# An attention and MLP block on one core: the next q asked for in step 2 of a unit, two maxima at the first score tile of every projection step, six pairs held back in one query block

## Chip, core and metric

One core of a Trainium2 chip runs the whole kernel. The metric is the device time of one execution in microseconds (us); the time of a kernel is the median of several executions.

## The reference, cut to what matters

An adaLN block: attention with 16 heads of 28 columns on 2048 tokens of 448 columns, then a channel MLP. Everything is float32.

```python
sa, ca, ga, sb, cb, gb = (mod[:, i] for i in range(6))      # mod = silu(c) @ w_mod
h = _layernorm(x) * (1 + ca) + sa
q, k, v = split(h @ wqkv)                                    # 16 heads of 28
p = softmax(q @ k.T * 28 ** -0.5)
x = x + ga * ((p @ v) @ wo)
h = _layernorm(x) * (1 + cb) + sb
x = x + gb * (gelu(_layernorm(h) @ w1 + b1) @ w2 + b2)
```

## The kernel before

**Phase 1** (to about 168 us) makes q, k and v. Each q and k is kept as two parts, a rounded one (hi) and the rest (lo), and stored in DRAM by group of 4 heads.

**Phase 2** is the attention and the subject here. It has 16 units (NU), unit u = 4 g + qt for head group g and query block qt of 512 queries, and each unit has 16 steps kt, one for each 128 keys; step s = 16 u + kt counts them through. A step makes two score tiles, each of two heads, by 12 matmuls (L1297: hi·hi, hi·lo, lo·hi), ScalarE takes the exponential of each tile (L1310), and the matmuls of the step before's probabilities with v follow (`av`, L1255). A head has 28 rows, so it sits in one of four groups of 32 rows of the TensorE array: the heads j = 0 and 1 of a group are the score tile of half 0, the heads 2 and 3 that of half 1.

The exponential needs each query's maximum before its unit begins. These **maxima** are the filler work of phase 2: a matmul of q and k by the hi parts (L476, row group j) and a VectorE reduction over its 512 keys (L481). 64 of them belong to a query block (4 sub-blocks i of queries, 4 heads j, 4 key chunks cch). The list `mxq` holds those that are left, and `emit_single(half, ...)` takes the next whose operands are there, by preference one of the asked half; a matmul in row groups that the score matmuls beside it don't use can run with them. What is taken, and so the row group, follows from the whole history of the list.

- Up to step 119 (RING) an even step takes two maxima at the first score tile (half 0, so heads 2 and 3 are asked for) and two at the second; an odd step one and two. `n0` (L1285) is the number at the first tile.
- **Pairs** save a reduction: `open_pair` makes the maximum of a difference of two key chunks (ScalarE, L641) in a buffer, `close_pair` (L648, VectorE) turns it into two maxima at once. Only heads 2 and 3 are paired; `PAIR_ROWS` says of how many of the 4 sub-blocks of a query block (the default is all 4, 8 pairs). `kept_back` holds the maxima of coming pairs away from `emit_single`.
- From step 119 on ("ring") a step takes one maximum at the first tile and two in one tile at the second: `emit_pair` looks for two heads of the asked half with the same i and cch, and reduces both at once (L684). If it finds none it makes two single ones in the same tile (L687, reduced at L481).
- The steps kt = 8 to 11 of units 12 to 15 are the **projection steps** (`is_wo`): each carries the output projection of 128 tokens (L396), and three maxima.

When the last maximum of a query block is done, `max_fin` folds them; **`put`** (L523) transposes them on VectorE (L525) and writes them by four small DMAs (L528) into the row of the unit's q tile that the scores read. It runs only when that q tile has been asked for: **`load_q`** (L777, two DMAs of 256 KB, hi and lo, recorded at L770). The hi parts for the maxima of the next head group (`kh`, `qh`) are loaded by `load_hi` (L508) when the last maximum that needs the old ones has been taken; the planner may use a loaded tile 3 steps later (L504).

All these DMAs stand in the one queue of **SyncE (SP)**, in program order, and SP waits at each until what it needs is there. In the same queue stand the DMAs of a unit's end: `den` (L998) in step 1 of the next unit, then `drec` (L1006) and its broadcast `osb` (L1008) in step 4 (step 2 in units 12 to 15), for which GpSimd (POOL) waits at L1013 to normalise; in units 12 to 15 the result goes by L1023 and L1024 into the projection steps.

Of the kernel before, what the change touches and what calls it, by code (L numbers as in the profile page):

```python
# [33 lines left out]
LAST_MAX = NKT - 4  # L34
RING = 119
PAIR_AT = (2, 2, 0, 2)
PAIR_ROWS = {(0, 2): 2, (0, 3): 3, (1, 0): 2, (1, 1): 2}
WO_MAX = 3
YTAGS = [f"{a}{i}" for a in ("kh", "qh") for i in range(4)]
EPS = 1e-5  # L40
# [4 lines left out]
def tile_adaln_block(ctx: ExitStack, tc: tile.TileContext, x, wqkv, wo, w1, b1, w2, b2, c, w_mod, out):  # L45
# [36 lines left out]
    def slot(tag, shape, dt=F32R):  # L82
        return sb.tile(shape, dt, tag="slot_" + tag, name=nm("slot_" + tag), bufs=1)
# [14 lines left out]
    def ps_two(key):  # L98
        return ps_pools[key][1].tile([128, 2, 512], F32, tag=key, name=nm(key), bufs=1)

    def ps_s2():
        s_ring.append(s_ring.pop(0))
        return ps_two(s_ring[-1])
# [4 lines left out]
    def ps_mx():  # L108
        mx_ring.append(mx_ring.pop(0))
        return ps_tile(mx_ring[-1], 1 if mx_ring[-1] == "m1" else 2)  # L110

    def ps_o():
        return ps_tile("o")
# [418 lines left out]
    def tick_late(force=False):  # L532
        for e in late:
            e[0] -= 1
        while late and late[0][2] in qst and (force or late[0][0] <= 0):
            late.pop(0)[1]()
# [74 lines left out]
    def other(m):  # L611
        return m[:2] + (m[2] + 1,) + m[3:]

    def pairable():
        return [
            m for m in mxq
            if m[2] == PAIR_AT[m[0]] and m[4] > 1 and other(m) in mxq and m[3] < PAIR_ROWS.get(m[:2], 4)
        ]
# [26 lines left out]
    def close_pair():  # L645
        (g, qt, cch, i, j), r = px_open.pop()
        p = max_mm(g, qt, i, j, kh_sb[(g, cch)])
        dve.tensor_tensor_reduce(  # L648
            out=r, in0=p, in1=r, scale=1.0, scalar=-3.0e38, op0=ALU.add, op1=ALU.max,
            accum_out=mxp[(g, qt)][:, i, j, cch + 1 : cch + 2],  # L650
        )
        count(g, qt, [cch, cch + 1])

    def emit_single(half, ps):
        near = ready_max()
        if not near:
            return
        whole = {}
        for m in near:
            whole[by_set(m)] = whole.get(by_set(m), 0) + 1  # L660
        fits = [m for m in near if m[4] // 2 == half]
        alone = [m for m in fits if whole[by_set(m)] == 1]
        same = [m for m in fits if m[:2] == near[0][:2]]
        m = (alone or same[-2:] or fits or near)[0]
        if clock[0] < RING:
            kept = kept_back()
            js = [e[0][4] for e in px_open]
            m = min(near, key=lambda x: (x in kept, x[4] // 2 != half, x[4] in js))
        mxq.remove(m)
        g, qt, cch, i, j = m  # L670
        max_one(g, qt, cch, i, j, ps)
        count(g, qt, [cch])

    def emit_pair(half, t):
        near = ready_max()
        for a, m in enumerate(near):
            n = m[:4] + (m[4] + 1,)
            if m[4] == 2 * half and n in near:
                mxq.remove(m)
                mxq.remove(n)  # L680
                g, qt, cch, i, j = m
                for jj in range(2):
                    max_mm(g, qt, i, j + jj, kh_sb[(g, cch)], lambda: t[:, jj])
                dve.tensor_reduce(out=mxp[(g, qt)][:, i, j : j + 2, cch], in_=t, op=ALU.max, axis=AX.X)  # L684
                count(g, qt, [cch, cch])
                return
        for jj in range(2):  # L687
            emit_single(half, lambda: t[:, jj])
# [36 lines left out]
    def finish_max(g, qt):  # L725
        if px_open and px_open[0][0][:2] == (g, qt):
            close_pair()
        while left[(g, qt)] > 0:
            emit_max(1)
# [35 lines left out]
    qst = {}  # L765
# [11 lines left out]
    def load_q(u):  # L777
        g, qt = divmod(u, NB)
        qst[u] = load_parts(f"b{u % 2}", 0, g, slice(qt * 512, (qt + 1) * 512))
# [136 lines left out]
    def third_tile(on):  # L916
        ps_close("m2" if on else "s2")
        ps_open("s2" if on else "m2", "right")
        mx_ring[:] = ["m1"] if on else ["m1", "m2", "m2"]
# [249 lines left out]
    NU = NG * NB  # L1169
# [61 lines left out]
    def is_wo(s_):  # L1231
        return s_ // NKT >= NU - NB and 8 <= s_ % NKT < 12

    def extra(s_):
        if is_wo(s_):
            return False
        most = 0
        need = 0
        for v in range(s_ // NKT + 1, NU):
            need += left.get(divmod(v, NB), 64)  # L1240
            rest = range(s_, NKT * (v - 1) + LAST_MAX)
            n_wo = sum(is_wo(x) for x in rest)
            n_plain = len(rest) - n_wo
            if n_plain > 0:
                most = max(most, (need - 3 * n_plain - WO_MAX * n_wo) / n_plain)
        due[0] += min(most, 1)
        if due[0] < 1:
            return False
        due[0] -= 1
        return True  # L1250
# [12 lines left out]
    for u in range(NU):  # L1263
        g, qt = divmod(u, NB)
        for kt in range(NKT):
            step = u * NKT + kt
            if kt == 6 and u + 1 < NU and u + 1 not in qst:
                load_q(u + 1)
            clock[0] = step
            if kt == LAST_MAX and u + 1 < NU:  # L1270
                finish_max(*divmod(u + 1, NB))
            tick_late()
            if not (three or mxq or late):
                three = True
                s_ring[:] = ["s0", turns[step % 2], turns[1 - step % 2]]
            now[0] = turns[step % 2]
            was, ring = ring, step >= RING and (three or not is_wo(step))
            first = step % 2 if ring else 0
            pt = {hf: slot(tags[step % len(tags)], [128, 2, 512], F32) for hf, tags in zip((first, 1 - first), ptags)}
            if ring != was:  # L1280
                third_tile(ring)
            more = ring and not three and extra(step)
            late_one, after = after, more
            n_max = 0 if ring else WO_MAX if is_wo(step) else 4 - step % 2
            n0 = 1 if step % 4 == 3 else 2  # L1285
            closing = bool(px_open) and step % 2 == 1

            ks, qs = kst[(g, kt // 4)], qst[u]
            kc = slice((kt % 4) * 128, (kt % 4 + 1) * 128)
            for n, hf in enumerate((first, 1 - first)):  # L1290
                s2 = ps_s2() if three else ps_two((now[0] if n else "s0") if ring else ("s1", "s0")[n if step < RING else 1 - n])
                for term, (kp, qp) in enumerate(((0, 0), (1, 0), (0, 1))):
                    if ring and n == 1 and term == 2 and mxq:
                        emit_pair(first, ps_two(turns[1 - step % 2]))
                    for jj in range(2):
                        rows_ = slice(64 * hf + 32 * jj, 64 * hf + 32 * jj + DH + (term == 0))
                        pe.matmul(s2[:, jj, :], ks[rows_, kp, kc], qs[rows_, qp, :], start=(term == 0), stop=(term == 2))  # L1297
                    if closing:
                        if (n, term) == (0, 0):
                            close_pair()  # L1300
                    elif n == 0 and term < n0 <= n_max:
                        emit_single(1, ps_mx)
                    if n == 1 and term == 2:
                        for _ in range(2 if closing else n_max - n0):
                            emit_single(0, ps_mx)
                    if ring and (n, term) == ((1, 0) if late_one else (0, 0)) and not three:
                        emit_single(1 - first, ps_mx)
                    if n == 1 and term == 2 and more:
                        emit_single(first, ps_mx)
                act.activation(pt[hf], s2, AF.Exp, scale=SCALE)  # L1310
            if step == 0:
                v_task(NB - 1, 3, ps_mx())
            if pend is not None:
                pu, pkt, pp, po = pend
                av(pu, pkt, pp, po)
                if pkt == NKT - 1:
                    end_unit(pu, po)
            if step % 2 and step + 2 < RING:
                open_pair()
            if kt == 0:  # L1320
                o = ps_o()
            pend = (u, kt, pt, o)
            if qt == NB - 1 and kt % 4 == 3 and g + 1 < NG:
                load_k(g + 1, kt // 4 if g else kt // 4 ^ 2)
            for fn in sched.pop(step, ()):
                fn()
# [115 lines left out]
```

## Time and profile before

| | us |
|---|---|
| median of 3 runs | 1121.79 |
| lowest and highest | 1120.84, 1122.47 |
| the profiled execution | 1122.83 |
| its span on the core | 1120.9 |
| phase 2, first score matmul to the start of the last step | 168.2 to 822.9 |

The profiled execution's own time is 1.93 us longer than its span, and 1.04 us above the median of the runs. In the rows that the prediction quotes a time is in us from the start of the span. A row of a timeline has start, duration, engine, line, operation, tile and source, the number of instructions merged into the row, and in brackets the idle time before it with what ended it. "SPq" rows are the issue of a DMA on SP. A row of a table of stretches has the stretch, its length, then for PE (matmuls), PEld (weight loads), DVE (VectorE), ACT (ScalarE) and POOL the busy time and the number of instructions, and then the clock that TensorE was granted, as a share of full speed, and the DMA load.

### The profile page before, as it was taken

The page shows a single profiled execution, that of the slowest core. Times are in us where ns is not written, and L with a number is a line of the kernel's source. Part 1 is how long each engine was busy: PE and PEld are TensorE (multiplying, and loading weights), DVE is VectorE, ACT ScalarE, POOL GpSimd, SP SyncE. Part 2 cuts the span into 40 slices and gives each one's busy share as a digit, 9 for nine tenths or more (in the row PEclk, how much of TensorE's full clock was granted, in tenths as well). Part 3 has the DMA queues.
Part 4 walks back from the last instruction along what each step waited for, and adds up shares of the span by engine and source line. Part 5 has one row for each costly group of instructions (what it writes and reads, how often), then busy time and mean ns, then how long its engine had stood idle before and what let it go on. Part 6 is the DMA issues. An engine that isn't in the chain of part 4 may idle for free.

```text
span 1120.9 us, 20683 instructions
## 1 busy us (share of the span) xinstructions
PE 1105.9 (99%) x8319; PEld 669.6 (60%) x8319; DVE 807.3 (72%) x1393; ACT 693.9 (62%) x878; POOL 214.9 (19%) x215
## 2 busy tenths in 40 slices
PE   9999999999999999999899999999999999999998
PEld 6756675444444444444344454545568888888887
DVE  6968788999989989988788867573648853444322
ACT  4555657888888888888788878576752311111210
POOL 2533333010000000000100020206214504023000
PEclk9999999999999999999999999999999999999999
DMA  8563263121132101231211412111322100000000
GB/s 309 200 200 93 88 201 112 31 86 33 56 114 59 57 30 58 58 87 58 76 40 39 143 30 87 57 30 58 91 69 78 31 33 1 1 33 1 33 1 33
DMA packets 49341, 81.19 MB, mean 72 GB/s; under 512 B 12311, under 2 KB 18702, under 8 KB 49234
## 3 DMA queue, kind: packets, MB, share of 16 engines
q1 hardware_dynamic: 48762, 79.14, 22.7%
q8 instruction: 65, 1.06, 0.4%
q10 hardware_dynamic: 148, 0.46, 0.1%
q0 software_dynamic: 336, 0.28, 0.1%
q14 instruction: 30, 0.25, 0.1%
HBM read 55.04 MB, written 26.48 MB: 73 GB/s over the span
## 4 chain that ended last, share of the span: by engine, by line
PE 92%; DVE 3%; DMA 2%; ACT 1%; issue 1%; SPq 0%; POOL 0%; DVEq 0%; ACTq 0%; POOLq 0%
PE s L1297 22%; PE o L1255 22%; PE m L396 16%; PE pa L396 8%; PE m L476 8%; PE s L1377 3%; PE s L1378 3%; PE s L1376 3%; DVE mxp L481 2%; PE s L476 2%; PE t L1377 1%; PE t L1378 1%; PE t L1376 1%; PE ma L476 1%; DMA slot_c<-in_w_mod_dram 1%
## 5 line engine op out<-in xcount | busy, mean ns | idle before, releaser
L481 DVE TENSOR_REDUCE mxp<-m 128x1 f32<-128x512 f32 x564 | 365.8, 686 | 87.4 <-PE m L476 68.6
L1297 PE MATMUL s<-slot_b,slot_a 28*128 28x512 f32 (+1 forms) x3072 | 360.0, 425 | 0.5 <-ACT slot_c0h L1310 0.5
L1297 PEld LDWEIGHTS s<-slot_b,slot_a 28*128 28x128 f32 (+1 forms) x3072 | 212.6, 184 | 172.5 <-ACT slot_c L1310 91.4
L476 PE MATMUL m<-kh,qh 28*128 28x512 f32 x598 | 222.0, 469 | 4.2 <-DMA kh<-d 3.3
L1310 ACT ACTIVATE slot_c<-s 128x1024 f32<-128x1024 f32 x170 | 174.8, 1028 | 57.8 <-PE s L1297 56.2
L1255 PE MATMUL o<-slot_c,v 128*32 128x512 f32 x680 | 179.6, 607 | 0.0
L1353 ACT ACTIVATE full<-m,b_col 128x512 f32<-128x512 f32 x56 | 38.6, 689 | 191.9 <-PE m L396 179.7
L1255 PE MATMUL o<-slot_c1h,v 128*32 128x512 f32 x512 | 136.3, 611 | 0.9 <-ACT slot_c1h L1310 0.9
L1255 PE MATMUL o<-slot_c0h,v 128*32 128x512 f32 x512 | 134.7, 605 | 0.0
L1310 ACT ACTIVATE slot_c0h<-s 128x1024 f32<-128x1024 f32 x128 | 131.4, 1026 | 3.4 <-PE m L396 2.4
L684 DVE TENSOR_REDUCE mxp<-s 128x2 f32<-128x1024 f32 x104 | 127.5, 1226 | 5.1 <-PE s L476 0.6
L1310 ACT ACTIVATE slot_c1h<-s 128x1024 f32<-128x1024 f32 x128 | 130.7, 1021 | 0.0
L1356 DVE CAST hi<-full 128x512 fp32r<-128x512 f32 x56 | 25.2, 450 | 135.1 <-ACT full L1353 135.1
L1310 ACT ACTIVATE slot_d<-s 128x1024 f32<-128x1024 f32 x86 | 88.3, 1027 | 29.1 <-PE s L1297 26.3
L476 PEld LDWEIGHTS m<-kh,qh 28*128 28x128 f32 x598 | 89.8, 182 | 20.6 <-DVE mxp L481 12.3
L1255 PE MATMUL o<-slot_d,v 128*32 128x512 f32 x344 | 91.4, 610 | 0.4 <-ACT osb L1219 0.4
L1013 POOL TENSOR_TENSOR osb<-osb,osb 128x512 f32<-128x512 f32 x16 | 20.9, 1306 | 365.7 <-DMA osb<-drec 306.0
L396 PE MATMUL m<-y,slot_a 128*128 128x512 f32 x160 | 60.7, 395 | 0.0
L648 DVE CUSTOM_DVE_ANT_0 slot_d0i<-m,slot_d0i 128x512 f32<-128x512 f32 x55 | 38.0, 691 | 15.2 <-PE m L476 12.8
L476 PE MATMUL s<-kh,qh 28*128 28x512 f32 x210 | 47.7, 441 | 0.8 <-DVE mxp L481 0.8
L1357 DVE TENSOR_TENSOR lo<-full,hi 128x512 fp32r<-128x512 f32 x56 | 44.1, 788 | 5.2
L1255 PEld LDWEIGHTS o<-slot_c,v 128*32 128x32 f32 x680 | 24.5, 108 | 39.0 <-issue 36.5
(342 smaller groups left out, 1845.6 us busy)
## 6 DMA issues: line engine op xcount, KB each, us to landing
slot_b<-d SPq DMA_DIRECT2D x32, 256.0 KB
slot_a<-d SPq DMA_DIRECT2D x32, 256.0 KB
d<-lo SPq DMA_DIRECT2D x28, 256.0 KB
d<-hi SPq DMA_DIRECT2D x16, 256.0 KB
osb<-drec SPq DMA_DIRECT2D x15, 256.0 KB
out_dram<-xn SPq DMA_DIRECT2D x16, 224.0 KB
raw<-in_B_w_dram SPq DMA_DIRECT2D x14, 224.0 KB
qh<-d SPq DMA_DIRECT2D x12, 256.0 KB
```

Source lines behind the costliest of these rows:

```text
L396: pe.matmul(p, a, b, start=(i == 0), stop=(i == len(terms) - 1))
L476: pe.matmul(m, qh_sb[(g, qt)][js, i * 128 : (i + 1) * 128], k[js, :], start=True, stop=True)
L481: dve.tensor_reduce(out=mxp[(g, qt)][:, i, j, cch : cch + 1], in_=m, op=ALU.max, axis=AX.X)
L684: dve.tensor_reduce(out=mxp[(g, qt)][:, i, j : j + 2, cch], in_=t, op=ALU.max, axis=AX.X)
L1255: pe.matmul(o[32 * j : 32 * j + 32, :], v_sb[kt // 4][:, kt % 4, 4 * g + j, :], p[j // 2][:, j % 2, :], start=(kt == 0), stop=(kt == NKT - 1),
L1297: pe.matmul(s2[:, jj, :], ks[rows_, kp, kc], qs[rows_, qp, :], start=(term == 0), stop=(term == 2))
L1310: act.activation(pt[hf], s2, AF.Exp, scale=SCALE)
L1353: act.activation(gf, p, AF.Gelu_apprx_tanh, bias=b1_col[:, i : i + 1])
L1357: dve.tensor_tensor(out=glo, in0=gf, in1=f(ghi), op=ALU.subtract)
L1376: pe.matmul(pp, ghi[:, ts], w_hi, start=(m == 0), stop=False)
L1377: pe.matmul(pp, ghi[:, ts], w_lo, start=False, stop=False)
L1378: pe.matmul(pp, glo[:, ts], w_hi, start=False, stop=(m == NFT - 1))
```

## The change

Three places are edited; no instruction of a new kind comes in.

```diff
-PAIR_ROWS = {(0, 2): 2, (0, 3): 3, (1, 0): 2, (1, 1): 2}
+PAIR_ROWS = {(0, 2): 2, (0, 3): 3, (1, 0): 2, (1, 1): 2, (1, 2): 3}
...
-            if kt == 6 and u + 1 < NU and u + 1 not in qst:
+            if kt == 2 and u + 1 < NU and u + 1 not in qst:
                 load_q(u + 1)
...
-            n0 = 1 if step % 4 == 3 else 2
+            n0 = 1 if step % 4 == 3 and not is_wo(step) else 2
```

The first holds back the pairs of 3 sub-blocks of the query block (1, 2), 6 pairs, where it were 8. The number of pairs in the program stays 55: block (1, 2) has two fewer, block (2, 2) three where it had one. But it changes what `emit_single` takes from step 54 on, and so the row groups, the steps in which query blocks are finished and those in which `load_hi` runs. Two maxima of heads 0 and 1 stand at the first tile (half 0, the same row groups) of steps 72, 74, 76 and 78 in the kernel before, and of steps 76 and 78 in the changed one; late in unit 14, maxima in the row groups of their tile stand in steps 229 to 232 before, and once, in step 233, after. The second edit moves `load_q`, and with it `put`, ahead of the unit's `drec`. The third changes steps 203 and 219 (kt = 11 of units 12 and 13) alone, since units 14 and 15 have no maxima left by then.

**SP's queue in unit 9** (steps 144 to 159). In the kernel before, from the unit's `den` on; `kh` and `qh` are hi parts of head group 3, `slot_b` with source `d` the q of unit 10 and with source `full` its `put`:

```order
L998 DMA den_7319<-osb_7287 128x1x16
L508 DMA kh_1804_7372<-d_244 128x512
L1006 DMA drec_7413<-den_7319 128x16
L1008 DMA osb_7415<-drec_7413 128x1x512
L770 DMA slot_b_1820_7446<-d_235 128x512
L770 DMA slot_b_1820_7446<-d_239 128x512
L528 DMA slot_b_1820_7446<-full_7449 4x4x32 x4
L508 DMA kh_1826_7463<-d_244 128x512
L508 DMA kh_1847_7566<-d_244 128x512
L508 DMA qh_1849_7571<-d_236 128x512
```

In the changed kernel the same place reads:

```order
L508 DMA kh_1776_7249<-d_244 128x512
L998 DMA den_7321<-osb_7287 128x1x16
L770 DMA slot_b_1793_7323<-d_235 128x512
L770 DMA slot_b_1793_7323<-d_239 128x512
L528 DMA slot_b_1793_7323<-full_7326 4x4x32 x4
L1006 DMA drec_7420<-den_7321 128x16
L1008 DMA osb_7422<-drec_7420 128x1x512
L508 DMA kh_1821_7446<-d_244 128x512
L508 DMA kh_1826_7463<-d_244 128x512
L508 DMA qh_1828_7468<-d_236 128x512
```

The q and its `put` now stand ahead of `drec` and `osb`, and the loads of `kh` directly behind `osb`. In the kernel before the first of the two late `kh` (kh_1826, chunk 3) is asked for in step 150 and first used in step 154; in the changed kernel chunk 2 (kh_1821) is asked for in step 149 and first used in step 152, chunk 3 in steps 150 and 157.

**PE in step 152** of the changed kernel, the first matmuls of the step:

```order
L1255 MATMUL o_7289<-slot_c0h_7456,v_230 32x512 x2
L1297 MATMUL s_1839_7522<-slot_b_1683_6822,slot_a_1639_6629 128x512 x2
L476 MATMUL m_1840_7525<-kh_1821_7446,qh_1400_5645 128x512
L1297 MATMUL s_1839_7522<-slot_b_1683_6822,slot_a_1639_6629 128x512 x4
L1297 MATMUL s_1841_7533<-slot_b_1683_6822,slot_a_1639_6629 128x512 x4
```

and in the kernel before, where the `kh` of that place is one of chunk 0 that was loaded long ago:

```order
L1255 MATMUL o_7289<-slot_c0h_7456,v_230 32x512 x2
L1297 MATMUL s_1837_7517<-slot_b_1711_6948,slot_a_1640_6631 128x512 x2
L476 MATMUL m_1838_7520<-kh_1749_7125,qh_1585_6374 128x512
L1297 MATMUL s_1837_7517<-slot_b_1711_6948,slot_a_1640_6631 128x512 x4
L1297 MATMUL s_1839_7528<-slot_b_1711_6948,slot_a_1640_6631 128x512 x4
```

The third row is the one that moved: the new `kh` is read by the third matmul of the step.

**DVE in unit 14**, steps 229 to 231 (kt = 5 to 7), in the kernel before, where the two single reductions (x2) of one score-sized tile are step 230's:

```order
L481 TENSOR_REDUCE mxp_9310<-m_2388_10076 128x1
L684 TENSOR_REDUCE mxp_9310<-s_2390_10089 128x2
L481 TENSOR_REDUCE mxp_9310<-m_2395_10108 128x1
L481 TENSOR_REDUCE mxp_9310<-s_2397_10121 128x1 x2
L481 TENSOR_REDUCE mxp_9310<-m_2401_10139 128x1
L684 TENSOR_REDUCE mxp_9310<-s_2403_10152 128x2
```

and in the changed kernel:

```order
L481 TENSOR_REDUCE mxp_9419<-m_2389_10079 128x1
L684 TENSOR_REDUCE mxp_9419<-s_2391_10092 128x2
L481 TENSOR_REDUCE mxp_9419<-m_2395_10108 128x1
L684 TENSOR_REDUCE mxp_9419<-s_2397_10121 128x2
L481 TENSOR_REDUCE mxp_9419<-m_2401_10138 128x1
L684 TENSOR_REDUCE mxp_9419<-s_2403_10151 128x2
```

The two single reductions became one over both banks. It is the only such place in either kernel.

## The prediction

> **What bounds the kernel.** I read the page's busy times first, then a table of stretches by unit, then TensorE's waits.
>
> ```profile
> span 1120.9 us, 20683 instructions
> PE 1105.9 (99%) x8319; PEld 669.6 (60%) x8319; DVE 807.3 (72%) x1393; ACT 693.9 (62%) x878; POOL 214.9 (19%) x215
> ...
> 490.00:525.90 35.90, 35.90 (x372) 15.46 (x368) 31.47 (x38) 31.43 (x34) 2.61 (x3) 1.00 0.23 68
> 525.90:567.00 41.10, 37.84 (x375) 16.12 (x371) 31.07 (x38) 31.41 (x34) 3.81 (x3) 0.96 0.20 59
> 567.00:602.80 35.80, 35.80 (x372) 15.40 (x368) 31.21 (x36) 31.37 (x34) 2.61 (x3) 1.00 0.13 39
> ...
> 683.70:701.60 17.90, 17.90 (x191) 7.65 (x187) 15.35 (x18) 15.76 (x18) 1.28 (x1) 1.00 0.18 47
> 731.10:752.40 21.30, 20.52 (x191) 8.80 (x187) 15.52 (x19) 15.86 (x18) 1.26 (x1) 0.92 0.15 40
> ```
>
> TensorE is busy almost throughout, so a change without less matmul work gains only where TensorE stands still or runs slower than it could. The stretches show two such places. Units 8, 9 and 10 do the same work, but unit 9 (the second row) takes 41.1 us where its neighbours take 35.9 and 35.8: **5.2 us** too many. The first 8 steps of unit 14 (last row) take 21.3 us where those of unit 13 take 17.9: **3.4 us** too many. Both have a clock below 1.00. TensorE's waits name the causes:
>
> ```profile
> PE m L476 <- DMA kh<-d: 3.3, 1, 3.3
> ...
> PE s L476 <- DVE mxp L481: 0.8, 1, 0.8
> ```
>
> One wait of 3.3 us for a `kh`, one of 0.8 for a reduction. The rest of the two excesses is the clock. In stretches of 3.41 us around the two waits:
>
> ```profile
> 546.25:549.66 3.41, 2.69 (x29) 1.07 (x25) 2.35 (x4) 2.65 (x3) 0.37 (x1) 1.00 0.09 28
> 549.66:553.08 3.42, 0.88 (x13) 0.76 (x13) 0.38 (x1) 0.11 (x1) 0.00 (x0) 1.00 0.69 207
> 553.08:556.49 3.41, 3.41 (x25) 1.25 (x23) 1.76 (x3) 1.83 (x2) 0.00 (x0) 0.50 0.00 0
> 556.49:559.90 3.41, 3.41 (x42) 1.26 (x34) 3.06 (x5) 2.88 (x4) 1.19 (x1) 1.00 0.13 46
> 744.22:747.64 3.42, 2.64 (x27) 1.28 (x23) 2.46 (x4) 2.29 (x4) 1.26 (x1) 1.00 0.22 65
> 747.64:751.05 3.41, 3.41 (x22) 1.54 (x15) 0.97 (x2) 1.01 (x1) 0.00 (x0) 0.50 0.00 0
> ```
>
> Half clock is granted for exactly one stretch, directly after one with 13 or 27 matmuls; 42 are usual (fourth row), and 29 (first row) had no penalty. A half-clock stretch does 25 matmuls for 42, a loss of 3.41 x (1 - 25/42) = 1.4 us at least; half of it, 1.7 us, is my value; the unit's excess less the wait, 5.2 - 3.3 = 1.9, is the upper end.
>
> **Part 1: the loads of unit 9 (first and second edit).** SP's queue there:
>
> ```profile
> 529.39 0.59 SPq L998 DMA_DIRECT2D den<-osb  x1
> ...
> 537.82 0.32 SPq L1006 DMA_DIRECT2D drec<-den  x1
> 539.23 0.55 SPq L1008 DMA_DIRECT2D osb<-drec  x1
> 539.83 0.95 SPq L770 DMA_DIRECT2D slot_b<-d  x2
> 545.74 2.28 SPq L528 DMA_DIRECT2D slot_b<-full  x4
> 548.07 0.91 SPq L508 DMA_DIRECT2D kh<-d  x2
> ...
> 552.20 0.46 PE L476 MATMUL m<-kh,qh 28*128 28x512 f32 x1 [3.26 <-DMA kh<-d]
> ```
>
> The `put` (L528) cannot issue until the q that it writes into has landed, 545.74 - 539.83 = 5.9 us; then its four issues take 2.3 us, and the `kh` behind them, asked for in step 150, issues at 548.07 and is used at 552.20. In the changed kernel `put` has been served by then: its q issues right behind `den`, at 529.39 + 0.59 = 529.98, and even at 5.9 + 2.3 us SP is free at 538.2, when `drec` is due anyway (537.82). So this wait goes. What is late next is the `kh` of chunk 2. It stands directly behind `osb`, in the place that the q's first DMA has above, so it issues at 539.83; a DMA in that place landed 5.9 us later, and 5.8 us later a unit earlier:
>
> ```profile
> 503.72 0.94 SPq L770 DMA_DIRECT2D slot_b<-d  x2
> 509.53 2.28 SPq L528 DMA_DIRECT2D slot_b<-full  x4
> ...
> 544.01 0.50 PE L1297 MATMUL s<-slot_b,slot_a 29*128 29x512 f32 x2
> ```
>
> That gives 545.7, and step 152, whose third matmul needs it, starts at 544.01: a **new wait of 1.7 us**. Its bounds: 0 if it lands in the 4.1 us that `kh` took without an `osb` ahead (548.07 to 552.20, with 539.83 giving 544.0), and 3.3, the old wait. I take 1.7, since the row that has `osb` ahead is the nearest. Behind the waiting matmul stand the rest of the step's scores, then ScalarE's exponentials: everything waits. In one stretch of 3.41 us this leaves TensorE 1.7 us, about 21 matmuls, fewer than the 27 that were followed by half clock; so I add 1.7 us of clock (0 to 1.9). Unit 9 then costs 3.4 where it cost 5.2: **-1.8 us**. Bounds: -5.2 (no wait, no clock) and 0.
>
> The Trainium skill ("TensorE: Matmul & The Clock Gate", Part 1: The HAM clock gate) speaks against the added clock: its array falls to half rate after at least one idle window of about 3.4 us. The rows agree with the 3.41 us window, but not with the idle time: 0.78 us of idling was enough in unit 14, so here the measurement decides. By that rule of the Trainium skill the sum below would be 1.7 us lower.
>
> **Part 2: unit 14.** In step 230 no two maxima fit one reduction, so two single ones share a tile:
>
> ```profile
> 746.06 0.69 DVE L481 TENSOR_REDUCE mxp<-s 128x1 f32<-128x512 f32 x1
> ...
> 746.80 0.49 PE L476 MATMUL s<-kh,qh 28*128 28x512 f32 x1 [0.78 <-DVE mxp L481]
> ```
>
> The second matmul waits for the reduction of the first (746.06 + 0.69 = 746.75), and the half-clock stretch follows. The changed kernel has the double reduction there, and the steps keep their usual row groups. The excess of 3.4 goes; in exchange step 233 has one maximum in its score tile's rows, 0.1 by part 3. **-3.3 us.** Bounds: -3.4, and -1.7 if half clock comes for another reason.
>
> **Part 3: row groups in unit 4.** A step with free row groups and two of the four with taken ones, from first score matmul to first score matmul:
>
> ```profile
> 340.84:343.62 2.78, 2.78 (x29) 1.36 (x25) 2.75 (x5) 2.75 (x4) 0.00 (x0) 1.00 0.18 49
> 350.97:353.90 2.93, 2.93 (x29) 1.70 (x26) 2.61 (x5) 2.93 (x4) 1.29 (x1) 1.00 0.15 48
> 356.13:359.07 2.94, 2.94 (x29) 1.68 (x25) 2.50 (x6) 2.87 (x4) 0.00 (x0) 1.00 0.02 6
> ```
>
> In the first VectorE is busy 2.75 of 2.78 us: it sets the pace. In the others it has slack, and TensorE makes the same 29 matmuls in 0.15 us more. Steps 72 and 74 lose the conflict, 76 and 78 keep it: 2 x 0.155 = **-0.3 us** (0 to -0.3).
>
> **Part 4: what costs nothing.** Pairs remain 55, so the work of VectorE and ScalarE is the same:
>
> ```profile
> L648 DVE CUSTOM_DVE_ANT_0 slot_d0i<-m,slot_d0i 128x512 f32<-128x512 f32 x55 | 38.0, 691 | 15.2 <-PE m L476 12.8
> ```
>
> The `put` transposes and folds keep their number and move within a unit; VectorE has slack in the ring (31.5 of 35.9 us), and before it they move from one even step to another. The third edit, by the steps kt = 10, 11 and 12 of unit 12:
>
> ```profile
> 665.76:669.93 4.17, 4.17 (x34) 2.58 (x34) 1.89 (x3) 2.47 (x3) 1.15 (x1) 1.00 0.00 0
> 669.93:674.07 4.14, 4.14 (x33) 2.60 (x32) 1.98 (x3) 2.48 (x3) 1.14 (x1) 1.00 0.02 8
> 674.07:676.94 2.87, 2.62 (x24) 1.03 (x23) 1.59 (x2) 1.88 (x3) 1.15 (x1) 1.00 0.85 263
> ```
>
> Two and one (first row) and one and two (second) take the same time, TensorE being busy throughout, so 0; bounds +0.1, and -0.5 if the 0.25 us of idling in the third row went with it in both units. `load_q` moves 512 KB ahead of `drec` and `osb` in every unit. In units 1 to 11 nothing waits for `osb` before step 10. In units 12 to 14 it leads to the projection:
>
> ```profile
> 642.16 0.59 SPq L998 DMA_DIRECT2D den<-osb  x1
> 645.99 0.32 SPq L1006 DMA_DIRECT2D drec<-den  x1
> ...
> 653.86 1.29 POOL L1013 TENSOR_TENSOR osb<-osb,osb 128x512 f32<-128x512 f32 x1 [22.05 <-DMA osb<-drec]
> ...
> 656.86 0.42 DVE L1023 CAST hi<-osb 128x512 fp32r<-128x512 f32 x1
> ```
>
> GpSimd is done at 655.15 and VectorE takes the result at 656.86: 1.7 us of cover. The q would issue behind `den`, at 642.75, and in 4.1 us be in by 646.9, a delay of `drec` of under 1 us, while `osb` no longer has a q behind it: 0.
>
> **Sum.** -1.8 - 3.3 - 0.3 = -5.4 us. On the profiled execution's 1122.83 that is 1117.4; the median of the runs stands 1.04 lower, so **1116.4 us**.
>
> **Rivals.** (a) *The new wait is followed by full clock*, because it falls across two stretches (0.85 us in each, as the 3.41 - 2.69 = 0.72 of the 29-matmul row): 1.7 less, **1114.7**. The idle window of the Trainium skill's page on the clock gate would lead to the same time. (b) *No new wait*, because without the q behind it `osb` is done sooner: the whole 5.2 goes, **1113.0**. For it speaks the bound of 4.1 us; against it that two 256 KB loads again follow `osb`. (c) *The `kh` wait is as long as before*, or two stretches of half clock follow it: unit 9 gains nothing, **1118.2**, and with one more half-clock stretch 1119.9. (d) *Slower: `osb` late in units 12 and 13.* If `drec` and `osb` come a whole q (5.9 us) later, VectorE stops at L1023, 5.9 - 1.7 = 4.2 us in each, TensorE starves for reductions, and half clock follows each: 2 x (4.2 + 1.7) = 11.8, less 5.4, **1128.2**. It decides from a lateness of 1.7 + 1.0 = 2.7 us on, where 2 x (1.0 + 1.7) eats the 5.4. Against it: the q has 3.2 us of lead over `drec` (642.75 to 645.99). (e) *The change gains nothing*: half clock moves to other places in units 9 and 14, **1121**.
>
> **Chances.** Forecast 0.48, (a) 0.17, (b) 0.14, (c) 0.11, (d) 0.05, (e) 0.05. A measurement of this kernel tells about 0.2%, 2.2 us, from no change, so faster means under 1119.5: the forecast, (a), (b) and nearly all of (c), 0.88; the same 0.07; slower 0.05. The range leaves out (d), (e) and the ends of (b) and (c): 1112.8 to 1119.6. The forecast's own is 1115.6 to 1117.6.
>
> **What would show it.** Unit 9: no wait of 3.3 us in step 154, SP's `put` before its `drec`, and a TensorE wait for `kh` of about 1.7 us in step 152 with one half-clock stretch behind it. Unit 14: 17.9 us for its first 8 steps, and no half clock. Steps 72 and 74: 2.78 us. A wait of TensorE or VectorE in steps 199 to 203, or a half-clock stretch outside unit 9, would prove it wrong.

## The result, and the profile after

The changed kernel takes **1116.36 us** in the median of 4 runs (1115.46 to 1116.52), the kernel before beside it 1121.77 (1120.84 to 1122.47): a ratio of 0.9946, 95% interval 0.9934 to 0.9958. The profiled execution took 1116.36 us with a span of 1114.3.

The page's first two lines, then a table of stretches of the changed kernel: unit 9, its step 152, the first 8 steps of unit 14, and steps 72 and 74. The columns are those of the tables above.

```profile
span 1114.3 us, 20698 instructions
...
PE 1101.0 (99%) x8319; PEld 667.1 (60%) x8319; DVE 806.9 (72%) x1392; ACT 693.2 (62%) x878; POOL 214.7 (19%) x215
...
526.30:563.58 37.28, 36.25 (x372) 15.57 (x368) 31.20 (x38) 31.30 (x34) 3.81 (x3) 1.00 0.22 65
544.37:547.99 3.62, 2.59 (x27) 1.10 (x23) 1.75 (x3) 1.94 (x3) 2.53 (x2) 1.00 0.24 78
727.93:745.84 17.91, 17.91 (x188) 7.61 (x184) 15.34 (x18) 15.78 (x18) 1.28 (x1) 1.00 0.16 47
351.74:354.52 2.78, 2.78 (x30) 1.32 (x27) 2.60 (x5) 2.78 (x4) 0.80 (x1) 1.00 0.31 74
356.77:359.54 2.77, 2.77 (x31) 1.39 (x27) 2.67 (x6) 2.77 (x4) 0.00 (x0) 1.00 0.03 6
```

TensorE does the same 8319 matmuls in 4.9 us less of busy time. Up to 3.4 us of that are the two stretches of 3.41 us at half clock, which are gone: every row above has 1.00, and the first half-clock stretch of this execution begins at 1113.81, behind the last matmul. Unit 9 went from 41.1 to 37.3 us, the first 8 steps of unit 14 from 21.3 to 17.9, steps 72 and 74 from 2.93 and 2.94 to 2.78 and 2.77. In the other direction, phase 2 begins at 169.1 us in this execution and at 168.2 in that of before; none of the edits is in phase 1.

SP's queue and the matmul that waits, in unit 9 of the changed kernel:

```profile
529.76 0.58 SPq L998 DMA_DIRECT2D den<-osb  x1
530.44 0.90 SPq L770 DMA_DIRECT2D slot_b<-d  x2
533.80 2.27 SPq L528 DMA_DIRECT2D slot_b<-full  x4
538.01 0.33 SPq L1006 DMA_DIRECT2D drec<-den  x1
539.43 0.56 SPq L1008 DMA_DIRECT2D osb<-drec  x1
540.03 0.95 SPq L508 DMA_DIRECT2D kh<-d  x2
...
545.90 0.46 PE L476 MATMUL m<-kh,qh 28*128 28x512 f32 x1 [1.03 <-DMA kh<-d]
```

The `put` (L528) now waits 3.4 us for its q (530.44 to 533.80) instead of 5.9, and is through before `drec`. The two `kh` issue directly behind `osb`, at 540.03, and the first is used 5.9 us later, at 545.90, after a wait of 1.03 us. That is TensorE's only wait for a `kh` left.

### The profile page after: what moved, and what is told of

The parts are those of the page before. It is cut to its first block, busy times and chain, and to the rows that moved or that the text cites. A ratio compares the mean times of both kernels' runs of the same rounds, so it can differ in the third digit from the quotient of the medians.

```text
span 1114.3 us, 20698 instructions
## 1 busy us (share of the span) xinstructions
PE 1101.0 (99%) x8319; PEld 667.1 (60%) x8319; DVE 806.9 (72%) x1392; ACT 693.2 (62%) x878; POOL 214.7 (19%) x215
## 4 chain that ended last, share of the span: by engine, by line
PE 93%; DVE 3%; ACT 1%; DMA 1%; issue 1%; SPq 0%; POOL 0%; DVEq 0%; ACTq 0%; POOLq 0%
PE s L1297 22%; PE o L1255 22%; PE m L396 16%; PE pa L396 9%; PE m L476 8%; PE s L1377 3%; PE s L1376 3%; PE s L1378 3%; PE s L476 1%; DVE mxp L481 1%; PE t L1377 1%; PE t L1378 1%; PE t L1376 1%; PE ma L476 1%; DMA slot_c<-in_w_mod_dram 1%
```

## The experiments

The granted clock that is given for single runs is their mean over the whole run: one stretch of 3.41 us at half clock lowers it by 0.0015. A half-clock stretch at the very end of an execution lowers it too: in the profile of the first edit alone (0.999) the only one lies in the last 1.9 us of the span, where TensorE has no work. So 0.999 doesn't yet speak of half clock in the attention.

### The first edit alone

```diff
-PAIR_ROWS = {(0, 2): 2, (0, 3): 3, (1, 0): 2, (1, 1): 2}
+PAIR_ROWS = {(0, 2): 2, (0, 3): 3, (1, 0): 2, (1, 1): 2, (1, 2): 3}
```

> The first edit alone (six pairs held back in block (1, 2)); q is still asked for in step 6. Theory A (unit 9 is a matter of when the kh are asked for and used): the kh of chunk 2 is again asked for in step 149 behind osb and used in step 152, so unit 9 shows the same wait of about 1.0 us there and none of 3.3 in step 154, its put sitting harmlessly before the kh of chunk 3, which is used in step 157; the first 8 steps of unit 14 take 17.9 us, steps 72 and 74 take 2.78. The whole gain comes: about 1116.4 us. Rival B (it was the earlier q that freed SP): the 3.3 us wait and its half clock stay in unit 9 and only unit 14 and unit 4 gain: about 1118 us.

Measured: 1116.01 us (6 runs, 1115.13 to 1118.09), ratio 0.9957, interval 0.9943 to 0.9971: the whole gain, as far as the intervals tell. Its SP queue, its wait, and its stretches for unit 9 and for the first 8 steps of unit 14:

```profile
538.31 0.55 SPq L1008 DMA_DIRECT2D osb<-drec  x1
538.96 0.43 SPq L508 DMA_DIRECT2D kh<-d  x1
539.44 1.05 SPq L770 DMA_DIRECT2D slot_b<-d  x2
545.45 2.28 SPq L528 DMA_DIRECT2D slot_b<-full  x4
548.13 0.33 SPq L508 DMA_DIRECT2D kh<-d  x1
...
544.84 0.46 PE L476 MATMUL m<-kh,qh 28*128 28x512 f32 x1 [1.07 <-DMA kh<-d]
...
525.23:562.53 37.30, 36.23 (x373) 15.56 (x370) 31.21 (x38) 31.30 (x34) 3.86 (x3) 1.00 0.22 65
726.84:744.72 17.88, 17.88 (x188) 7.64 (x184) 15.35 (x18) 15.76 (x18) 1.29 (x1) 1.00 0.18 47
```

The q and its `put` still stand in the way of the second `kh` (548.13, as late as before), but nobody needs it until step 157. The first `kh` goes ahead of the q, and costs the same 1.0 us as in the changed kernel. Theory A holds: for unit 9 the first edit needs no earlier q.

### The second edit alone

```diff
-            if kt == 6 and u + 1 < NU and u + 1 not in qst:
+            if kt == 2 and u + 1 < NU and u + 1 not in qst:
```

> The second edit alone (q asked for in step 2). The kh of chunk 3 is asked for in step 150 and used in step 154 as in the kernel before, but SP has served the put by then. Theory A: it issues near 540.5 behind osb, lands near 546.3 and step 154 starts at 548.4: no wait, unit 9 takes 35.9 us, while unit 14 keeps its two single reductions and 21.3 us for its first 8 steps, and steps 72 and 74 keep 2.93. About 5 us less in the profile, 1117 us. Rival B (the chunk 3 load is late whoever stands ahead of it in SP): the wait stays at 2 us or more, about 1120 us.

Measured: 1118.00 us (8 runs, 1116.68 to 1119.44), ratio 0.9965, interval 0.9952 to 0.9979. Unit 9 and the first 8 steps of unit 14:

```profile
526.43:562.36 35.93, 35.93 (x374) 15.49 (x370) 31.17 (x38) 31.27 (x34) 3.82 (x3) 1.00 0.22 68
726.47:746.16 19.69, 18.91 (x189) 8.16 (x185) 15.53 (x19) 15.87 (x18) 1.27 (x1) 1.00 0.15 43
```

Unit 9 has no wait at all: the earlier q cures it more fully than the first edit does. So the two edits cure the same stall, and together they leave the 1.0 us that the first brings, because it makes a `kh` due one step sooner after its load (3 steps, not 4). Unit 14 keeps its trouble, at 19.7 us in this execution, 21.3 in that of before: the profile fell on one of the 3 runs with a granted clock of 1.000; the other 5 of the 8 had 0.998 or 0.996.

### The third edit alone

```diff
-            n0 = 1 if step % 4 == 3 else 2
+            n0 = 1 if step % 4 == 3 and not is_wo(step) else 2
```

> The third edit alone (two maxima at the first tile of steps 203 and 219). Theory A: those steps stay at 4.15 and 4.79 us, units 9 and 14 keep their excess, within 0.5 us of the kernel before: 1121.8. Rival B (the order inside the projection step matters): steps 203 and 219 or the ones behind them (2.87, 2.88) get shorter by 0.25 us or more each, about 1121.2.

Measured: 1121.96 us (10 runs, 1120.46 to 1122.52), ratio 1.0001, interval 0.9992 to 1.0010. Unit 9 with three stretches of 3.41 us in it, the steps 203 and 219, and the first 8 steps of unit 14:

```profile
526.66:568.10 41.44, 38.96 (x372) 16.61 (x368) 31.17 (x38) 31.25 (x34) 3.82 (x3) 0.92 0.20 59
...
548.31:551.72 3.41, 1.35 (x10) 0.20 (x5) 1.41 (x2) 1.66 (x2) 0.00 (x0) 1.00 0.44 112
551.72:555.14 3.42, 3.00 (x21) 1.45 (x21) 1.92 (x2) 1.74 (x2) 0.00 (x0) 0.50 0.33 123
555.14:558.55 3.41, 3.41 (x27) 1.42 (x23) 1.15 (x2) 1.08 (x2) 0.00 (x0) 0.50 0.00 0
...
671.09:675.25 4.16, 4.16 (x34) 2.57 (x33) 1.89 (x3) 2.47 (x3) 1.15 (x1) 1.00 0.02 8
717.89:722.69 4.80, 4.80 (x38) 3.20 (x37) 1.89 (x3) 2.48 (x3) 1.15 (x1) 1.00 0.14 26
...
732.21:751.68 19.47, 18.69 (x189) 8.07 (x186) 15.53 (x19) 15.86 (x18) 1.28 (x1) 1.00 0.15 43
```

4.16 and 4.80, where before 4.15 and 4.79 stood: for the steps and the time theory A holds. Unit 9 keeps its excess, but in another mixture: the wait was 2.5 us here, with 6.8 us at half clock behind it, where before it was 3.3 with 3.4. Unit 14 kept 1.6 us of its excess, at full clock.

The edit doesn't stay within the steps 203 and 219, as was said under the change: it alters the order of the maxima after them too, up to step 233. In steps 229 to 231 the kernel before has four maxima in the row groups of their tile, this one has two. The two single reductions in step 230 remain.

### osb of unit 8 from another queue

The changed kernel with one place more; `drec` and `osb` of that unit are issued by GpSimd:

```diff
         def t_rec():
-            q_ = pool if u == NU - 1 else sp
+            q_ = pool if u in (8, NU - 1) else sp
```

> The changed kernel, with drec and osb of unit 8 (the ones in step 148) issued from GpSimd's queue in place of SP's; no other place. Theory A (the kh of chunk 2 is late because it stands behind osb in one queue): it issues from SP as soon as its old tile is free, near 538.5, lands near 543 and step 152 has no wait: unit 9 takes 36.0 us in place of 37.3, about 1.3 us less than the changed kernel, 1115.1. Rival B (the 256 KB loads share the DMA engines, whatever queue they come from): it lands near 545.7 as before and the wait of about 1.0 us stays, 1116.4. Rival C: osb from GpSimd comes so late that L1013 and the matmuls behind it wait; there is no such wait before step 155.

Measured: **1114.81 us** (5 runs, 1114.40 to 1115.32), ratio 0.9942, interval 0.9929 to 0.9955. SP, GpSimd, and unit 9:

```profile
539.02 1.78 SPq L508 DMA_DIRECT2D kh<-d  x2
...
540.92 0.71 POOL L1008 DMA_DIRECT2D osb<-drec  x1 [1.70 <-DMA drec<-den]
...
548.26 1.28 POOL L1013 TENSOR_TENSOR osb<-osb,osb 128x512 f32<-128x512 f32 x1 [6.52 <-DMA osb<-drec]
...
526.45:562.37 35.92, 35.92 (x373) 15.43 (x369) 31.17 (x38) 31.42 (x34) 5.42 (x6) 1.00 0.23 68
```

The `kh` issue 1.0 us sooner and ahead of `osb`; the wait is gone, and unit 9 takes 35.9 us. GpSimd has `osb` at 548.26, and TensorE doesn't wait for that. The `kh` both left its place behind `osb` and started earlier. The trace's semaphore updates part the two: the last part of this `kh` is in at 541.9, 2.9 us after its issue, where in the changed kernel it took 5.7 (540.03 to 545.8). So most of what it gained is that it no longer stands behind `osb`, as theory A has it. Rival B isn't refuted for all loads: the second `kh`, issued at 540.48 and followed 0.4 us later by `osb` from the other queue, took 5.2 us. It is not needed until step 157.

### The kh of chunk 2 used one step later

```diff
-        loaded[(kind, g, b)] = clock[0] + 3
+        loaded[(kind, g, b)] = clock[0] + (4 if (kind, g, b) == (1, 3, 2) else 3)
```

> The changed kernel, where the planner may use the kh of chunk 2 of group 3 four steps after its load in place of three: it is used from step 153 on, and nothing else of the order changes. Theory A (the wait is the time from the load to its first use): it lands near 545.8 and step 153 starts at 546.6, so the wait of 1.0 us goes without any change of queue, as with osb issued from GpSimd: unit 9 takes 35.9 us, 1115.0 us. Rival B (something else in unit 9 is late as well and then ends last): a wait of 0.5 us or more stays, 1115.8 or more.

Measured: 1115.19 us (5 runs, 1114.86 to 1115.57), ratio 0.9936, interval 0.9923 to 0.9948, beside 15 runs of the kernel before with a median of 1122.84. Unit 9:

```profile
526.65:562.59 35.94, 35.94 (x372) 15.53 (x368) 31.20 (x38) 31.43 (x34) 3.81 (x3) 1.00 0.23 68
```

The wait goes without any change of queue: it was the distance from load to first use, as theory A has it. The ratios of this run and the last can't be told from the changed kernel's, since the intervals overlap; what the wait costs, 1.3 to 1.4 us, is read from unit 9.

### The first edit with osb of unit 8 from the other queue

The first edit and the `t_rec` line above, without the second and third edits.

> The first edit alone with drec and osb of unit 8 from GpSimd's queue; q in step 6 and n0 as before. Theory A (the gain is the first edit's; the other two edits give nothing): the same time as the changed kernel with that queue, 1114.8 us, unit 9 at 35.9 to 36.2. Rival B (the earlier q gives something once the wait for chunk 2 is away): 0.5 us or more above it, 1115.4 or more.

Measured: **1114.44 us** (5 runs, 1114.29 to 1115.44), ratio 0.9931, interval 0.9918 to 0.9944; unit 9 takes 35.95 us. This is the shortest median of all, with the first edit alone of the three; from the version with all three (1114.81) it cannot be told. Once the wait for the `kh` is gone, the earlier q and the third edit add nothing.

### A long wait on purpose

The changed kernel with the `kh` of chunk 2 loaded twice:

```diff
-        sp.dma_start(f(t), f(dscr[kind][0][g])[:, b * 512 : (b + 1) * 512])
+        for _ in range(2 if (kind, g, b) == (1, 3, 2) else 1):
+            sp.dma_start(f(t), f(dscr[kind][0][g])[:, b * 512 : (b + 1) * 512])
```

> The changed kernel with the load of the kh of chunk 2 issued twice, one behind the other, so that it lands later by one load (3 to 4 us; the output stays the same). It makes the wait in step 152 as long as the one that the kernel before had. Theory A (a wait of over 3 us is followed by half clock in most executions, one of 1 us in few): wait of 4 us, granted clock at or under 0.998 in most runs, 1116.4 + 3.5 + 1.5 = about 1121. Rival B (half clock comes from something else in the kernel before): 1.000 in most runs, about 1119.9.

Measured: 1121.28 us (11 runs, 1119.78 to 1121.92), ratio 0.9987, interval 0.9978 to 0.9995; the wait is 3.5 us, and the granted clock is 0.998 or 0.997 in all 11 runs. The steps 152 and 153, then the three stretches of 3.41 us around the wait:

```profile
544.27:552.10 7.83, 4.34 (x27) 1.62 (x24) 2.08 (x3) 2.56 (x3) 2.53 (x2) 0.70 0.33 102
552.10:555.13 3.03, 3.03 (x28) 1.39 (x25) 1.60 (x2) 1.34 (x2) 0.00 (x0) 0.65 0.00 0
...
543.97:547.38 3.41, 0.80 (x6) 0.18 (x2) 0.46 (x1) 0.92 (x2) 1.26 (x1) 1.00 0.34 83
547.38:550.79 3.41, 2.53 (x17) 1.44 (x21) 1.52 (x2) 1.26 (x2) 1.27 (x1) 0.50 0.45 160
550.79:554.21 3.42, 3.42 (x27) 1.31 (x23) 1.08 (x2) 1.10 (x2) 0.00 (x0) 0.50 0.00 0
```

The two steps take 10.9 us, where the ring's usual pair takes 4.4: 6.4 us for a wait of 3.5, with 6.8 us at half clock behind it. One wait of this length costs most of the gain: the run is 6.1 us above the kernel that uses this `kh` one step later (1115.19), measured in the same rounds. Theory A holds. The stretch ahead of the half clock was not idle throughout: TensorE did 0.80 us of matmuls in it.

### Two single reductions in step 230, alone

The changed kernel, with `emit_pair` kept from finding a pair in that step:

```diff
-        for a, m in enumerate(near):
+        for a, m in enumerate(near if clock[0] != 230 else ()):
```

> The changed kernel with two single reductions in one tile forced in step 230, as in the kernel before, but without its maxima in taken row groups in steps 229, 231 and 232. Theory A (the two single reductions alone are the cost of unit 14): the first 8 steps of unit 14 take 19.5 us with full clock and 21.2 with a half-clock stretch, about 1118 us with half clock in about half of the runs. Rival B (the taken row groups around them make a good part): 18.5 us or less and 1.000 in all runs, about 1117.

Measured: 1117.39 us (5 runs, 1116.80 to 1118.18), ratio 0.9956, interval 0.9941 to 0.9971, granted clock 1.000 in all 5 runs. The first 8 steps of unit 14, and TensorE's wait:

```profile
727.80:746.82 19.02, 18.24 (x190) 7.79 (x186) 15.48 (x19) 15.85 (x18) 1.26 (x1) 1.00 0.15 44
...
PE s L476 <- DVE mxp L481: 0.8, 1, 0.8
```

Neither theory holds as written. The two reductions cost 19.0 - 17.9 = 1.1 us with the same wait of 0.8 us, not 1.6, and no half clock follows. With the second edit alone, which leaves the order of the maxima as it was before, the same place took 19.7 us at full clock: the 0.7 us between go with its four maxima in taken row groups in steps 229 to 231, and with two of them (the third edit alone, 19.5 us) it was 0.45.

Half clock was seen in this place only with them, in the profiled execution of before. The lower clock in 5 of 8 runs of the second edit, against none of 5 here, fits that, but it is few runs, and without a trace it isn't shown where in them the half clock lay. A rival stays open: where the wait falls. In the profile of this run it is spread over two stretches of 3.41 us (0.3 and 0.5 us of idling), in that of before it lies in one.

## Why the prediction was right, point by point

- **What bounds the kernel:** right. The gain is in the two places that the table by unit showed, 3.8 us in unit 9 and 3.4 in unit 14, and 0.45 in unit 4.
- **Part 1, the old wait:** right in its mechanism. The 3.3 us wait behind `put` is gone, and the second edit alone removes it by the earlier `put`. But that edit was not needed: with the first alone the late `kh` isn't due until step 157, and the same 3.8 us come.
- **Part 1, the new wait:** right in its place and cause: step 152, behind `osb`, issue at 540.03 (forecast 539.83), landing before 545.90 (545.7). The term was too large: 1.7 us forecast, 1.03 of idling measured and 3.62 - 2.28 = 1.34 for the step. The 1.7 counted from the start of the step; its first two score matmuls still ran, to 544.87, and the step itself began at 544.37, not 544.01.
- **Part 1, the clock behind it:** the term that was mis-sized, 1.7 us forecast, none measured. With the wait it makes unit 9's gain 2.0 us larger than forecast. Rival (a) had full clock here, but for a reason that did not come true: it put the wait across two stretches, and the wait (544.87 to 545.90) lies whole in one. That stretch,

```profile
543.78:547.19 3.41, 2.38 (x27) 1.10 (x23) 1.54 (x3) 1.73 (x3) 1.85 (x2) 1.00 0.43 127
547.19:550.61 3.42, 3.42 (x38) 1.33 (x32) 2.94 (x3) 3.04 (x4) 0.68 (x1) 1.00 0.00 0
```

  has 27 matmuls, as many as the one in unit 14 of the kernel before that was followed by half clock, and less busy time (2.38 against 2.64), yet 1.00 follows. So the number of matmuls, from which I argued, does not decide. The rule of the Trainium skill that I set aside ("TensorE: Matmul & The Clock Gate", Part 1: The HAM clock gate) was the nearer here: a wait of 3.5 us, about its window of 3.4, went with a lower granted clock in 11 of 11 runs, one of 1.0 us in at most 1 of the 10 runs of the changed kernel and the first edit alone (a run at 0.998) and in none of the 5 with the single reductions in step 230. As it stands the rule isn't borne out either: no stretch ahead of half clock in the attention was idle throughout. They had 0.80 us of matmuls with the long wait, 0.88 in unit 9 before, 1.35 there with the third edit, and 2.64 in unit 14 before.
- **Part 2, unit 14:** right, 17.9 us, though not all of its 3.4 us was the two reductions: 1.1 go with them, 0.7 with the taken row groups, the rest is the clock. That the half clock follows from the wait of 0.8 us alone, as this part had it, isn't borne out: with the same wait it stayed away in the profiles of the second edit, of the third edit and of the single reductions alone.
- **Part 3:** right, 2.78 and 2.77 us where 2.78 was forecast. Unit 4 gained more in step 70 (2.92 to 2.77), which no part of the forecast had; with the second edit alone that step takes 2.79 too. **Part 4:** right; steps 202 to 204 read as before,

```profile
662.58:666.75 4.17, 4.17 (x34) 2.57 (x34) 1.89 (x3) 2.47 (x3) 1.15 (x1) 1.00 0.00 0
666.75:670.89 4.14, 4.14 (x33) 2.57 (x32) 1.89 (x3) 2.47 (x3) 1.15 (x1) 1.00 0.02 6
670.89:673.76 2.87, 2.62 (x24) 1.05 (x23) 1.59 (x2) 1.88 (x3) 1.19 (x2) 1.00 0.84 250
```

  and no wait came in the projection steps, so rival (d) has nothing for it.
- **The sum:** 1116.4 forecast, 1116.36 measured. That it is this close is luck: three errors cancel. Between the two profiled executions the fall is 1122.83 - 1116.36 = 6.5 us, where the forecast had 5.4: unit 9 gave 2.0 more, while phase 2 began 0.9 us later. And the forecast took 1.04 us off because the profiled execution of before lay that much above its median; that of the changed kernel lies on its own. Between the medians the fall is 5.4, because the profiled execution of before, with its two half-clock stretches, lies above most: of 34 runs of the kernel before beside the experiments 5 had a granted clock of 1.000 (1119.11 to 1120.23 us), 12 of 0.998 (median 1121.74) and 17 less (median 1123.04). The changed kernel's runs had 1.000 or 0.999. So part of what the median gained is that it no longer runs at half clock. How long the wait of unit 9 is in those 5 runs at full clock no trace shows: they lie only about 3 us above the changed kernel, less than the waits of the profiled execution would give.

## What to carry to other kernels

Where one engine is busy 99% of the span, cut the span into stretches of equal work and look for the one that is longer: two waits, of 3.3 and 0.8 us, and the clock behind them were most of the gain here. A load is late by what stands ahead of it in its queue: moving the broadcast ahead of it to another queue, or using the load one step later, was worth the same 1.3 to 1.4 us of unit 9. When two edits of a change can cure the same stall, run each alone: one of the three carried it all.

## What the runs showed of the hardware

- Half clock comes in stretches of 3.41 us, on a fixed grid within an execution: the beginnings in the kernel before, 553.08 and 747.64, are 57 such stretches apart. (In the changed kernel the grid is counted back from its half-clock stretch at 1113.81.)
- Whether half clock follows goes, in these runs, nearly by how long TensorE computes in a stretch. In the nine traces that show the grid, from 10 us on, every full-clock stretch with 0 to 1.35 us of matmuls was followed by half clock, and every one with 2.2 us or more by full clock, but for one: that of unit 14 before, with 2.64 us. The stretch of the same wait with the third edit alone had 2.64 too and kept full clock, so why this one did not is open. That matmuls in taken row groups count for less is a guess; no run measures it.
- A half-clock stretch was followed by another where TensorE idled in it (2.53 us of matmuls with the long wait, 3.00 with the third edit alone), and by full clock where it was busy throughout (3.41 us, four of four in unit 9 and unit 14). So the end of a wait matters beside its length: 2.5 us that reached into the next stretch cost two stretches at half clock, 3.3 us that ended before it cost one.
- A 256 KB load directly behind the broadcast `osb` took 5.1 to 6.2 us from its issue to its last semaphore update in eight traces. Ahead of `osb` in time, a `kh` took 2.9 and 3.2 us in the two runs where GpSimd issues `osb`; with no `osb` ahead of its q, the `put` could issue 3.4 us after it.
